# Three edits to the order of work in a fused attention and mixture-of-experts kernel: loads of k and q eight slots later, one maximum's scores ahead of the scores, the first expert's conversion later and sparser

## The chip, the cores and the metric

The kernel runs on one core of one Trainium2 chip. The metric is the device time of one execution in microseconds (us); the time before is the median of three runs. A core has five engines with a queue of instructions each: TensorE (PE, with its weight loads as PEld), VectorE (DVE), ScalarE (ACT), GpSimd (POOL) and SyncE (SP). Each executes its own instructions in their order and waits on semaphores for the others. ACT, POOL and SP also issue DMA transfers from their queues (ACTq, POOLq and SPq in the rows).

## What is computed

Masked attention over 2 batches and 8 heads (768 rows, 64 columns), then a dense layer pair with a smooth activation, then eight experts, of which each row goes to one:

```python
mask = q_bucket[:, :, :, None] == k_bucket[:, :, None, :]     # 6 sign bits of q@proj and k@proj
scores = np.where(mask, q @ k.T / 8, -1e9)
attn = exp(scores - max(scores)); attn /= attn.sum(-1) + 1e-9
x = (attn @ v)                       # as 1536 rows of 512
h = x @ w_in                         # 512 -> 2048
x = (h * tanh(log1p(exp(h)))) @ w_out
expert = argmax(normalised x @ normalised expert_emb.T)
out[row] = gate[row] * (relu(x[row] @ w1[expert]) @ w2[expert])
```

## The kernel before

Almost everything is float32 in the reference; the kernel splits each operand into two float16 parts (hi and lo) and multiplies three pairs of them on TensorE.

**Attention (from the start to about 249 us).** `run_all` walks over 16 heads. A head has six key tiles of 128 keys, and a key tile has six slots, so a head has 36 slots. All work is put at a slot number counted from slot 0 of its head; the table `AT` holds these numbers, negative ones lying in the heads before. For head n:

- `load_kq` (slot -190, now -182; every second head from the seventh on) loads k and q of two heads, two DMAs of 384 KB, from ACT's queue. `hi` (slot -150) is the first reader: an ACT instruction (L286) that writes the tile `ka`.
- `in_x` (slot -116) transposes `ka` to the tile `tx` by one DMA from SP's queue, and `args` (slot -91, L320, 12 matmuls into a PSUM tile `ar`) is its first reader. `in_m` (slot -84) transposes a tile `kq` to `tm` by a DMA from SP's queue too; the first reader is the head's first maximum unit. `load_v` (slot -37) loads v of two heads from SP's queue.
- `max_unit` computes scores for the row maxima: one matmul of 512 columns (L382) into a PSUM tile `ms`, reduced by DVE (L383, `mx`), and for every second pair of tiles two matmuls of 256 columns (L386, L387). They run ten key tiles ahead of the head's own scores. The PSUM pool `ps_m` has two buffers, which `ms` and `ar` take in turn.
- `score_unit` computes one key tile's scores: four matmuls (L422 from `tx`, L424 from `tm`) and one exponential on ACT (L427, tile `p`).
- `pv` multiplies with v, three key tiles later (L444, or L442 for the tiles that are split into two float16 parts). `out` copies a finished half to SBUF on ACT (L467, L469).

In the key tile named `first` in the code, the sixth one of a head's `pv`, slot 1 held: `pv` of the first half, `out`, the score unit of the next head, then the first maximum unit of the head three after. Such a tile comes once in each head.

Beside the heads, the weights of the dense layer are converted (`w1_work`): DVE shifts and merges them in three steps per block (L749, L751, L731), ACT rounds (L758, L759, or L765) and POOL or DVE (L766) makes the low part, into `wi` and `wo`.

**Dense layers (about 249 to 505 us).** `moe1` walks over 48 groups G, 16 for each third of the rows. In group G, PE multiplies 12 matmuls for a later group's `h` (L818, `up`), then 12 for the output of the group three before (L877). ACT and DVE evaluate the activation in between: ACT L896 (reads `h`), L901, L907, L910, then DVE L919, ACT L925, DVE L898 and L903 (the last reader of `h`), ACT L912 (`g`), POOL L913. Two PSUM buffers hold `h` in the second half of the walk, so L818 of one group waits for L903 of the group two before. After each third, ACT and DVE cut the output into parts (L949, L950, in the list `new`), and `route` follows: 16 DMA transposes from SP's queue, matmuls for the logits (L974), DVE's choice of an expert (L1012 to L1017), and a counting matmul on PE (L1025).

Side work is handed out in steps by `fill`: `every` gives how many steps stand at three places of a group (`FILL0` is 0, 3, 3, and `FILL` 0, 4, 2, so six in a group). First in the line is the rest of `w1_work`, then `w2_work`, which converts the first expert: 16 pieces, `a_0` in eight (from the loads 0 and 1) and `b_0` in eight (from the loads 2 and 3), each an ACT instruction (L1159) and a DVE instruction (L1160), one piece every `W2LAG` steps. The loads `st` come from SP's queue, into two buffers. ACT's part of a piece is put in the list `later` and issued in the middle of a group.

**Experts (about 505 us to the end).** Not touched by the change.

Of the kernel before, what the change touches and what calls it, by code (L numbers as in the profile page):

```python
# [36 lines left out]
PRE = {96: 2, 97: 2, 98: 2}  # L37
RPB, CVB = 1, 3
STEP = 7
AT = dict(rows_t=-7, rows_in=-7, m_row=-22, bits=-90, max_end=-24, hi=-150, lo0=-130, lo1=-122, dup=-114, in_x=-116, in_m=-84, args=-91, load_kq=-190, load_v=-37, out0=50, out1=54, s_row=55, inv=77, r_out=79, r_in=91, scale=112, v16=18, p16=(9, 13), xhi=127, xlo=139)  # L40
GAP = dict(bits=1, max_end=1, inv=1)
STEPS = dict(bits=3, max_end=2, inv=2)
FROM = dict(v16=2, p16=2, rows_in=1, m_row=4, bits=3, max_end=1, hi=4, lo0=4, lo1=4, dup=4, in_x=4, in_m=4, rows_t=1, args=3, load_kq=6, load_v=2)
# [3 lines left out]
SP, MP, OP = 1, (1, 5, 11), (1, 5)  # L47
# [100 lines left out]
class Attn:  # L148
# [364 lines left out]
    def run_all(self, bs, hook=None):  # L513

        seq = [(b, h) for b in bs for h in range(H)]
        N = len(seq)

        self.load_v(0, 0)
        self.load_kq(0, 2)
        act, dve = self.nc.scalar.copy, self.nc.vector.tensor_copy  # L520
        Z, pools, copies, its = self.Z, dict(s=self.ps_s, o=self.ps_o, m=self.ps_m), dict(a=act, d=dve), {}
        for line in PRO:
            f, *x = line.split()
            b, h = seq[int(x[0])] if x and f[:4] != "warm" else (0, 0)
            if f == "warm":
                self.warm(int(x[0]))
            elif f == "warm_s":
                self.warm(int(x[0]), self.ps_s.tile([P, 2, 512], F32, tag="s", name="warmed")[:, 0, 0:HS])
            elif f == "proj":
                self.proj()  # L530
            elif f == "kq":
                self.load_kq(b, h)
            elif f in ("x", "m"):
                (self.out_x if f == "x" else self.out_m)(b, h, self.turn_pe, pools[x[1]], x[1])
            elif f in ("cx", "cm"):
                Z[b, h][f](int(x[1]), copies[x[2]])
            elif f == "dup":
                self.dup(b, h, copies[x[1]])
            elif f == "args":
                self.args(b, h, pools["o"] if x[1] == "o" else None, *(int(y) for y in x[2:]))  # L540
            elif f in ("bits", "max_end"):
                if (f, h) not in its:
                    its[f, h] = getattr(self, f)(b, h)
                next(its[f, h], None)
            else:
                getattr(self, f)(b, h, *(int(y) for y in x[1:]))
        todo = {}

        def put(n, at, f, *args):
            todo.setdefault(n * NJ * 6 + at, []).append(partial(f, *seq[n], *args))  # L550

        def steps(n, f, *ats):
            def one(b, h):
                it.append(it.pop() if it else f(b, h))
                next(it[0], None)

            it = []
            for at in ats:
                put(n, at, one)

        for n in range(N):
            for name, at in AT.items():
                if n == 3:
                    at = AT3.get(name, at)
                if n == N - 1 and name in LAST:
                    continue
                if n < FROM.get(name, 0) or n >= UNTIL.get(name, N) or n % EVERY.get(name, (1, 0))[0] != EVERY.get(name, (1, 0))[1]:
                    continue
                if name == "p16":
                    for t in T16:  # L570
                        for u in range(2):
                            put(n, 6 * t + at[u], self.p16, t, u)
                elif name in GAP:
                    d = GAP[name]
                    steps(n, getattr(self, name), *(at + i * d for i in range(STEPS[name])))
                elif name == "dup":
                    put(n, at, self.dup, copies[DUPE])
                elif name in ("lo0", "lo1"):
                    put(n, at, self.lo, int(name[2]))
                elif name in ("in_x", "in_m"):  # L580
                    put(n, at, self.turn_in, name[3])
                else:
                    put(n, at, getattr(self, name))
        for k, f in (("x", self.out_x), ("m", self.out_m)):
            put(3, AT3[k], f, self.turn_pe, self.ps_m, "m")
            for i in range(2):
                copy = copies[CP3[k == "m"][i]]
                put(3, AT3[f"c{k}{i}"], lambda b, h, k, i, copy: Z[b, h]["c" + k](i, copy), k, i, copy)
        put(3, AT3["dup"], self.dup, dve)
        for g in range(G0, TEND + 1):  # L590
            n, t = divmod(g, NJ)
            m, j = divmod(g + MXL, NJ)
            p, u = divmod(g - PVL, NJ)
            if g < NJ:
                n, t = (0, S0.index(g)) if g in S0 else (-1, 0)
            if g < PVL + NJ:
                p, u = (0, O0.index(g)) if g in O0 else (-1, 0)
            for pos in range(6):
                first = g >= NJ + PVL and 0 <= p < N and u == NJ - 1
                if pos == SP and first:  # L600
                    self.pv(*seq[p], u, 0)
                    self.out(*seq[p], 0)
                if pos == SP and 0 <= n < N:
                    self.score_unit(*seq[n], t)
                if 0 <= m < N and j % 2 * 6 + pos in MP:
                    i = MP.index(j % 2 * 6 + pos)
                    self.max_unit(*seq[m], j // 2 * 2 + (i > 0), int(i == 2))
                if pos in OP and 0 <= p < N and not (first and pos == OP[0]):
                    self.pv(*seq[p], u, OP.index(pos))
                for f in todo.get(6 * g + pos, ()):  # L610
                    f()
            if hook:
                hook(g)
# [25 lines left out]
NR = CH // P  # L639
GLAG = 3  # L640
FILL = (0, 4, 2)
FILL0, SLOW = (0, 3, 3), 18
XIN = 2
AHEAD = 21
W2LAG = 6
R0, NC = 7, 10
EARLY = 48
WARM2 = (2, 2)
# [7 lines left out]
class Moe:  # L656
# [176 lines left out]
    def moe1(self, side, more):  # L833

        nc, tm = self.nc, self.tm
        N = NT // CH * NF1
        h, m, g, cuts, new = self.h, {}, {}, [], []
# [18 lines left out]
        for G in range(N + GLAG):  # L856
# [3 lines left out]
            elif G < N:  # L860
                t, w, u = m[G] = [T(tag, G) for tag in "twu"]
            new_g = 0 < G < N
            every = FILL0 if G < SLOW else FILL
            cuts, new = new[NC:], []
            ups = [2, 3, 4, 5] if G == 0 else [G + 2] if 4 <= G <= AHEAD + 1 else [G] if AHEAD + 3 < G < N else []
            if G > AHEAD:
# [2 lines left out]
            if G >= GLAG:  # L869
# [8 lines left out]
                if f == NF1 - 1:  # L878
                    route = self.route(c, x2, late, delayed)
                    if c < NT // CH - 1:  # L880
                        side.append([now + R0, route])
                        new = next(route)
# [28 lines left out]
            if old:  # L911
                nc.scalar.copy(g[G - 1][:, 0, :], p1)  # L912
                nc.gpsimd.tensor_tensor(g[G - 1][:, 1, :], p1, g[G - 1][:, 0, :], op=ALU.subtract)  # L913
            while self.later:
                self.later.pop(0)()
            for x in new[:NC]:
                x(0)
# [406 lines left out]
def moe_attn(ctx, tc, a):  # L1324
# [9 lines left out]
    with ExitStack() as c1:  # L1334
# [45 lines left out]
        with ExitStack() as c2:  # L1380
# [14 lines left out]
            with in_order(tc, last):  # L1395
                moe.busy = True
                moe.moe1([chain(work, moe.w2_work(*W[2:], W2LAG))], more)
    with ExitStack() as c2:
# [40 lines left out]
```

## Time and profile before

| what | value |
|---|---|
| time before, median of three runs | 683.24 us (682.69 to 684.28) |
| the profiled execution's own time | 685.03 us |
| its span, first to last instruction | 683.1 us |
| PE busy | 661.0 us, 97% of the span |
| ACT busy | 483.7 us, 71% |
| DVE busy | 474.7 us, 69% |
| POOL busy | 166.5 us, 24% |
| mean granted TensorE clock | 0.995 of full speed |

The profiled execution has 1.93 us around its span, and lies 1.79 us above the median of the three runs. A matmul's record includes its way through the array, so PE reads as busy over short waits: a wait shorter than about 0.16 us between two matmuls doesn't show as idle time and has to be read from the start times.

### The profile page before, as it was taken

To read this page: it belongs to the slowest core of one execution; us is meant where nothing else is said; L and a number is where in the kernel's file an instruction comes from. 1 tells how busy PE (TensorE), PEld (TensorE's weight loads), DVE (VectorE), ACT (ScalarE), POOL (GpSimd) and SP (SyncE) were. 2 spreads that over 40 slices of the span, in tenths; PEclk is the share of its full clock that TensorE was granted. 3 is DMA by queue.
4 is the path that set the end of the run, shared out by engine and by line. 5 is a ranking of instruction groups with operands and counts; after the bars stand their busy time and mean duration, and the time that the engine had idled before them with its cause. 6 is when DMAs were issued, how large, how long until landed. Compare 5 with 4: busy or idle time off the path is not lost. (4 is left out here: it accounts for less than half of the span.)

```text
span 683.1 us, 10667 instructions
## 1 busy us (share of the span) xinstructions
PE 661.0 (97%) x3946; PEld 377.8 (55%) x3946; DVE 474.7 (69%) x784; ACT 483.7 (71%) x735; POOL 166.5 (24%) x226
## 2 busy tenths in 40 slices
PE   8899999899999999999999999999999999999995
PEld 4555555455555554444444444445467777667772
DVE  7868899799988669998685665545566655566620
ACT  5667787687776779899997888887754655556530
POOL 4122122130221222322342342422522011001011
PEclk9999999999999999999999999999999999999998
DMA  7264775958563223474035010310355999999600
GB/s 222 61 144 125 154 178 132 182 142 200 126 133 109 72 76 117 123 203 152 2 94 153 1 63 0 90 36 1 103 193 167 266 280 311 265 265 259 182 23 22
DMA packets 119772, 92.72 MB, mean 136 GB/s; under 512 B 86788, under 2 KB 99076, under 8 KB 119714
## 3 DMA queue, kind: packets, MB, share of 16 engines
q1 hardware_dynamic: 111442, 80.65, 44.9%
q0 software_dynamic: 2240, 6.31, 3.4%
q10 hardware_dynamic: 6032, 5.01, 2.6%
q8 instruction: 33, 0.54, 0.4%
q14 instruction: 25, 0.20, 0.1%
HBM read 63.44 MB, written 14.24 MB: 114 GB/s over the span
## 5 line engine op out<-in xcount | busy, mean ns | idle before, releaser
L818 PE MATMUL h<-xx,wi 128*128 128x512 f16 x576 | 131.3, 379 | 0.7 <-DVE w L903 0.6
L877 PE MATMUL x<-wo,g 128*128 128x512 f16 x576 | 131.3, 379 | 0.5 <-DVE w L903 0.5
L444 PE MATMUL o<-p,vn 128*65 128x384 f32 (+3 forms) x272 | 109.4, 488 | 0.3 <-ACT su L469 0.3
L427 ACT ACTIVATE p<-s 128x768 f32<-128x768 f32 x96 | 76.8, 805 | 29.6 <-PE s L424 28.8
L877 PEld LDWEIGHTS <-g 128*128 128x128 f16 x576 | 56.3, 98 | 68.7 <-issue 0.8
L818 PEld LDWEIGHTS <-wi 128*128 128x128 f16 x576 | 56.1, 98 | 67.8 <-issue 1.1
L913 POOL TENSOR_TENSOR g<-w,g 128x512 f16<-128x512 f32 x47 | 56.9, 1210 | 148.9 <-ACT g L912 94.0
L1218 PE MATMUL y<-b,hh 128*128 128x512 f16 (+1 forms) x384 | 84.2, 379 | 0.0
L1204 PEld LDWEIGHTS <-a 128*128 128x128 f16 x768 | 75.0, 98 | 6.7 <-issue 1.6
L383 DVE TENSOR_REDUCE mx<-ms 128x1 f32<-128x512 f32 x96 | 65.3, 686 | 15.8 <-PE ms L382 15.2
L1204 PE MATMUL h<-xt,a 128*128 128x240 f16 x672 | 70.5, 266 | 1.1 <-DMA xt<-xs 1.1
L919 DVE SCALAR_TENSOR_TENSOR w<-w,u 128x512 f32<-128x512 f32 x47 | 32.4, 690 | 46.3 <-ACT u L910 44.1
L1218 PEld LDWEIGHTS <-hh 128*128 128x128 f16 (+1 forms) x384 | 43.7, 114 | 37.6
L702 DVE SCALAR_TENSOR_TENSOR b<-st,b 128x1024 f16<-128x1024 f32 x28 | 33.1, 1222 | 31.0 <-ACT b L701 31.0
L444 PEld LDWEIGHTS o<-p,vn 128*65 128x65 f32 (+1 forms) x272 | 42.5, 164 | 18.6 <-issue 8.2
L1224 POOL DMA_INDIRECT out_dram<-o,row x16 | 16.4, 1028 | 144.5 <-ACT o L1223 124.4
L424 PE MATMUL s<-tm 97*128 97x384 f16 x192 | 47.4, 327 | 0.0
L702 DVE SCALAR_TENSOR_TENSOR a<-st,a 128x1024 f16<-128x1024 f32 x28 | 34.3, 1223 | 18.8 <-ACT a L701 18.8
L422 PE MATMUL s<-tx 128*128 128x384 f16 x192 | 47.1, 327 | 0.0
L898 DVE SCALAR_TENSOR_TENSOR t<-t,u 128x512 f32<-128x512 f32 x47 | 37.8, 805 | 12.6 <-ACT t L925 12.6
L1223 ACT ACTIVATE o<-y,row 128x512 f32<-128x512 f32 (+1 forms) x16 | 11.0, 686 | 42.8 <-PE y L1218 22.8
L387 DVE TENSOR_REDUCE mx<-ms 128x2 f32<-128x512 f32 x48 | 32.9, 685 | 10.0 <-PE ms L386 9.5
(207 smaller groups left out, 1065.8 us busy)
## 6 DMA issues: line engine op xcount, KB each, us to landing
st<-in_moe_w_dram SPq DMA_DIRECT2D x32, 1024.0 KB, 5.9
stg<-in_moe_w_in_dram SPq DMA_DIRECT2D x16, 512.0 KB, 4.2
stg<-in_moe_w_out_dram SPq DMA_DIRECT2D x16, 512.0 KB, 4.2
xs<-zrow SPq DMA_DIRECT2D x15, 257.0 KB, 6.6
vn<-in_v_dram SPq DMA_DIRECT2D x16, 192.0 KB, 5.3
rb<-rd SPq DMA_DIRECT2D x14, 192.0 KB, 3.6
xr<-row SPq DMA_DIRECT2D x2, 1024.0 KB, 5.5
kq<-in_k_dram ACTq DMA_DIRECT2D x5, 384.0 KB, 4.4
```

The source lines that it names most:

```text
L383: nc.vector.tensor_reduce(z["mx"][:, j, 0:1], s, axis=AX.X, op=ALU.max)
L422: nc.tensor.matmul(s[:, c, :], kq[:, 0, ts], kq[:, 1, c * HS : (c + 1) * HS], start=True, stop=False)
L424: nc.tensor.matmul(s[:, c, :], m[0:97, 0, ts], m[0:97, 1, c * HS : (c + 1) * HS], start=False, stop=True)
L427: nc.scalar.activation(p[:, 0:S].rearrange("p (c n) -> p c n", c=2), s, AF.Exp, scale=2.0**-11)
L444: nc.tensor.matmul(o, self.vn(b, h, t), z["p"][t][:, cs], start=(t == 0), stop=(t == NJ - 1))
L702: nc.vector.scalar_tensor_tensor(lo, src, sc, hi, op0=ALU.mult, op1=ALU.subtract)
L818: self.nc.tensor.matmul(h, self.wi[wu][:, k, fs], x[:, k, xs], start=(i == 0), stop=(i == 3 * NKT - 1))
L877: nc.tensor.matmul(x2[r], gf[:, gu, rs], self.wo[wu][:, f, :], start=(f == 0 and gu + wu == 0), stop=(f == NF1 - 1 and gu == 1))
L898: nc.vector.scalar_tensor_tensor(t1, t1, 0.75, u1, op0=ALU.add, op1=ALU.mult)
L913: nc.gpsimd.tensor_tensor(g[G - 1][:, 1, :], p1, g[G - 1][:, 0, :], op=ALU.subtract)
L1204: nc.tensor.matmul(h[:, v, :], W[0][wu][:, k, fs], xt[e][:, xu * NKT + k, :], start=(i == 0), stop=(i == 3 * NKT - 1))
L1218: nc.tensor.matmul(y[s][0 : CS[s].stop - CS[s].start], hs[F // 2][:, hu, F % 2, CS[s]], W[1][wu][:, F, :], start=(F == 0 and hu + wu == 0) ...
```

## The change

Three edits. `load_kq` goes from slot -190 to -182. In the tile named `first`, the maximum unit goes ahead of the score unit. In `moe1`, the first two groups hand out no steps of side work (`QUIET`), a piece of the first expert comes every eight steps and not every six (`W2LAG`), and ACT's part of a piece isn't issued in a group that cuts an output (`not new`).

```diff
-AT = dict(rows_t=-7, rows_in=-7, m_row=-22, bits=-90, max_end=-24, hi=-150, lo0=-130, lo1=-122, dup=-114, in_x=-116, in_m=-84, args=-91, load_kq=-190, load_v=-37, out0=50, out1=54, s_row=55, inv=77, r_out=79, r_in=91, scale=112, v16=18, p16=(9, 13), xhi=127, xlo=139)
+AT = dict(rows_t=-7, rows_in=-7, m_row=-22, bits=-90, max_end=-24, hi=-150, lo0=-130, lo1=-122, dup=-114, in_x=-116, in_m=-84, args=-91, load_kq=-182, load_v=-37, out0=50, out1=54, s_row=55, inv=77, r_out=79, r_in=91, scale=112, v16=18, p16=(9, 13), xhi=127, xlo=139)
...
                     self.pv(*seq[p], u, 0)
                     self.out(*seq[p], 0)
-                if pos == SP and 0 <= n < N:
+                if pos == SP and 0 <= n < N and not first:
                     self.score_unit(*seq[n], t)
                 if 0 <= m < N and j % 2 * 6 + pos in MP:
                     i = MP.index(j % 2 * 6 + pos)
                     self.max_unit(*seq[m], j // 2 * 2 + (i > 0), int(i == 2))
+                if pos == SP and 0 <= n < N and first:
+                    self.score_unit(*seq[n], t)
...
-FILL0, SLOW = (0, 3, 3), 18
+FILL0, QUIET, SLOW = (0, 3, 3), 2, 18
...
-W2LAG = 6
+W2LAG = 8
...
-            every = FILL0 if G < SLOW else FILL
+            every = (0, 0, 0) if G < QUIET else FILL0 if G < SLOW else FILL
...
-            while self.later:
+            while self.later and not new:
                 self.later.pop(0)()
```

The instructions are the same in number on every engine. From L643 on, a line of the changed kernel has a number higher by two. The first place is ACT's queue in the seventh head, around the loads of the 13th and 14th (`kq_1_4`). Before:

```order
L427 ACTIVATE p_171<-s_6_4_1532 128x768
L276 DMA kq_1_4_1543<-in_k_dram 128x2x384
L276 DMA kq_1_4_1543<-in_q_dram 128x2x384
L758 ACTIVATE wi_102<-cv_6_1416 128x4x128
L759 ACTIVATE cv_6_1416<-cv_6_1416 128x512
L307 COPY kq_159<-ka_2_1396 128x12x64
L286 ACTIVATE ka_3_1556<-kq_1_2_1236 128x2x6x64
L427 ACTIVATE p_171<-s_6_5_1558 128x768
L427 ACTIVATE p_172<-s_7_0_1578 128x768
```

And now:

```order
L427 ACTIVATE p_171<-s_6_4_1532 128x768
L760 ACTIVATE wi_102<-cv_6_1416 128x4x128
L761 ACTIVATE cv_6_1416<-cv_6_1416 128x512
L307 COPY kq_159<-ka_2_1396 128x12x64
L286 ACTIVATE ka_3_1553<-kq_1_2_1256 128x2x6x64
L427 ACTIVATE p_171<-s_6_5_1555 128x768
L276 DMA kq_1_4_1565<-in_k_dram 128x2x384
L276 DMA kq_1_4_1565<-in_q_dram 128x2x384
L427 ACTIVATE p_172<-s_7_0_1578 128x768
```

The two loads stand behind five more ACT instructions, right after the exponential of the head's last key tile. On SP's queue nothing moves in the attention.

The second place is PE in a tile named `first`, where `pv` of the seventh head (`o_6`) ends, the eighth head's scores are made (`s_7_2`), and the maxima of the tenth begin (`ms_1_0_0` and `ms_1_1_0`, of batch 1). Before:

```order
L442 MATMUL o_6_0_1512<-p_183,vh_178 65x384
L422 LDWEIGHTS tx_7_1079
L422 MATMUL s_7_2_1619<-tx_7_1079 128x384
...
L424 MATMUL s_7_2_1619<-tm_7_1223 128x384
L382 LDWEIGHTS tm_1_1530
L382 MATMUL ms_1_0_0_1626<-tm_1_1530 128x512
...
L382 MATMUL ms_1_1_0_1632<-tm_1_1530 128x512
```

And now:

```order
L442 MATMUL o_6_0_1512<-p_183,vh_178 65x384
L382 LDWEIGHTS tm_1_1530
L382 MATMUL ms_1_0_0_1620<-tm_1_1530 128x512
L422 LDWEIGHTS tx_7_1079
L422 MATMUL s_7_2_1623<-tx_7_1079 128x384
...
L424 MATMUL s_7_2_1623<-tm_7_1223 128x384
...
L382 MATMUL ms_1_1_0_1632<-tm_1_1530 128x512
```

One matmul of 512 columns goes ahead of four of 384. DVE's order is the same in the whole attention; this happens in 12 heads.

The third place is ACT in group 24 of `moe1`, behind the square of a route (`sq_2`). Before:

```order
L912 CAST g_3961<-w_3917 128x512
L957 ACTIVATE sq_2_3906,ss_3682<-sq_2_3906 128x512
L1159 ACTIVATE b_0_2897<-st_0_3860 128x2x256
L925 ACTIVATE t_3946<-w_3947,bias_77 128x512
L896 ACTIVATE t_3975<-h_9_3978 128x512
```

And now:

```order
L914 CAST g_3951<-w_3907 128x512
L959 ACTIVATE sq_2_3898,ss_3676<-sq_2_3898 128x512
L1161 ACTIVATE a_0_2895<-st_0_3790 128x512
L927 ACTIVATE t_3936<-w_3937,bias_77 128x512
L898 ACTIVATE t_3965<-h_9_3968 128x512
```

The piece of the third load (`b_0`) that stood here is now a piece of the second (`a_0`); the first one of `b_0` stands in group 29, and the last in group 39, where it was 31. In the groups 16 to 25 ACT had ten pieces and has six now, and one rounding of `wo` more.

## Rows read from the trace of the kernel before

**Rows 1.** PE's waits: line, waited for: us in total, times, longest us.

```profile
PE ms L382 <- DMA tm<-kq: 2.0, 1, 2.0
```

**Rows 2.** Timeline, 117 to 129 us: start, us, engine, line, operation [idle before].

```profile
116.96 1.88 SPq L263 DMA_TRANSPOSE tm<-kq  x1
...
117.46 0.44 ACTq L276 DMA_DIRECT2D kq<-in_k_dram  x1
...
118.93 5.54 SPq L263 DMA_TRANSPOSE tx<-ka  x1
...
128.92 0.63 PE L382 MATMUL ms<-tm 96*128 96x512 f16 x2 [1.97 <-DMA tm<-kq]
```

**Rows 3.** Page, part 6: DMA issues, median us from issue to landing.

```profile
tx<-ka SPq DMA_TRANSPOSE x12, 5.3
```

**Rows 4.** Tile tx, 118 to 119 us: landing of its one transpose.

```profile
DMA to landing us min/median/max: 11.2/11.2/11.2
```

**Rows 5.** Tile kq, 117 to 119 us: landing of the two loads.

```profile
DMA to landing us min/median/max: 8.7/9.0/9.3
```

**Rows 6.** One window: busy time of PE, PEld, DVE, ACT, POOL, granted clock, DMA.

```profile
129.00:134.00 5.00, 5.00 (x28) 2.63 (x29) 3.77 (x10) 2.48 (x4) 0.00 (x0) 0.66 1.04 229
```

**Rows 7.** Timeline, a tile named first, 143 to 145 us.

```profile
143.18 0.49 PE L422 MATMUL s<-tx 128*128 128x384 f16 x2
...
143.75 0.16 DVE L395 TENSOR_REDUCE m<-mx 128x6 f32<-128x12 f32 x1
143.84 0.59 PE L382 MATMUL ms<-tm 96*128 96x512 f16 x2
...
144.25 0.69 DVE L383 TENSOR_REDUCE mx<-ms 128x1 f32<-128x512 f32 x1 [0.35 <-PE ms L382]
...
144.60 0.33 PE L442 MATMUL o<-p,vh 128*128 128x385 f16 x1
...
145.00 0.45 PE L320 MATMUL ar<-pj,tx 128*128 128x18 f16 x12
```

**Rows 8.** Timeline, the same place in three other heads.

```profile
73.07 0.40 PE L320 MATMUL ar<-pj,tx 128*128 128x18 f16 x10
...
86.23 0.69 DVE L383 TENSOR_REDUCE mx<-ms 128x1 f32<-128x512 f32 x1
...
199.51 0.34 PE L320 MATMUL ar<-pj,tx 128*128 128x18 f16 x8
```

**Rows 9.** All waits: ACT's for the scores.

```profile
ACT p L427 <- PE s L424: 28.8, 40, 1.9
```

**Rows 10.** Timeline, start of the dense layers.

```profile
259.95 1.65 DVE L731 SCALAR_TENSOR_TENSOR cv<-stg,cv 128x512 uint32<-128x512 uint32 x1
...
263.26 4.69 PE L877 MATMUL x<-wo,g 128*128 128x512 f16 x21 [0.50 <-DVE w L903]
```

**Rows 11.** Timeline, the first route, 367 to 388 us.

```profile
367.40 1.08 SPq L1141 DMA_DIRECT2D st<-in_moe_w_dram  x2
...
373.34 0.63 ACT L1159 ACTIVATE b<-st 128x512 f16<-128x512 f32 x1 [3.12 <-DMA st<-in_moe_w_dram]
...
381.15 2.75 PE L818 MATMUL h<-xx,wi 128*128 128x512 f16 x12 [0.62 <-DVE w L903]
...
387.47 0.17 PE L1025 MATMUL rk<-oh,tri 128*128 128x8 f16 x1 [0.97 <-DVE oh L1017]
```

**Rows 12.** Timeline, a group with a piece, and a group of the second route.

```profile
411.30 0.60 ACT L896 ACTIVATE t<-h 128x512 f32<-128x512 f32 x1 [0.61 <-PE h L818]
...
443.87 0.69 DVE L903 SCALAR_TENSOR_TENSOR w<-t,h 128x512 f32<-128x512 f32 x1
...
445.01 2.75 PE L818 MATMUL h<-xx,wi 128*128 128x512 f16 x12
```

**Rows 13.** Line 766: count, ns min/median/max, first and last start us.

```profile
L766 DVE SCALAR_TENSOR_TENSOR wo<-cv,wo x8: 691/1379/1472, 256.5 to 320.4; 128x512 f16<-128x512 f32 x8
```

**Rows 14.** Timeline of PE, the 16th group's second product.

```profile
337.74 1.46 PE L877 MATMUL x<-wo,g 128*128 128x512 f16 x6
```

## The prediction, made before the changed kernel ran

> **What bounds the kernel now.** TensorE does. The first view is the table of busy time: PE at 97% of the span, ACT and DVE near 70%. So a change can gain only where PE waits, or where its clock is low, and the second view is the list of PE's waits. Beside one at the program's start, its longest entry is a single wait of 2.0 us for the transpose `tm<-kq` [rows 1]; no other wait is over 1.0 us. The third view is the timeline at that wait: the transpose was issued at 116.96, and PE's matmul that reads it began at 128.92 after 1.97 us idle [rows 2]. The fourth is a window right behind it: over the 5.00 us from 129 to 134 the granted clock was 0.66 on average [rows 6], so part of that stretch ran at the lower of the two levels (1.2 GHz, against 2.4) after PE had stood still. Waits too short for the list are found by start times: in a tile named `first`, the last matmul of `pv` starts at 144.60, its kind takes 0.16 us from start to start, and `ar` starts only at 145.00, right after DVE's reduction of `mx` ends (144.25 + 0.69 = 144.94) [rows 7]. That is 0.24 us lost. The same place shows it in nine heads, of which the first and the last stand in [rows 8]. In the dense layers PE waits at 263.26 for 0.50 us, at 381.15 for 0.62 and at 387.47 for 0.97 [rows 10, 11], each time for DVE.
>
> All terms below come from the profiled execution: span 683.1 us, 685.03 us with what lies around it. The median of the three runs is 1.79 us lower. The first term is a late transfer, and it may be smaller in the timed runs. It can't be wholly absent there: without it the profiled execution would come to 681.3, below the lowest run (682.69). The other reading is that a profiled execution is simply longer by 1.8. I sum against 685.03 and keep the other reading for the low end.
>
> **The loads of k and q.** From 73.07 to 199.51 lie nine heads [rows 8], 126.44 us, or 122.7 without the stall and its slow stretch (1.97 + 1.70, below). That is 13.6 us for a head and 0.379 for a slot, so eight slots are 3.0 us. Before, the two loads were issued at 117.46, half a microsecond after `tm` and ahead of `tx` (118.93) [rows 2]. They took 8.7 and 9.3 us to land [rows 5], and `tx` took 11.2 [rows 4] where the median of its twelve is 5.3 [rows 3]. SP's queue was held too: the issue of `tx` alone took 5.54 us [rows 2]. Now `tm` and `tx` are both issued before the loads, which come at about 120.5. `tm` is due 10.0 us after its issue (128.92 - 1.97 - 116.96); a transpose that isn't disturbed needs about half of that.
>
> What goes: the idle 1.97 us, and of the slow stretch 5.00 x (1 - 0.66) = 1.70 us. Together 3.7. What is late next: `tx` is due 25 slots after its issue, 9.5 us, with the loads now beside its second half; and the loads themselves are due 32 slots after theirs, 12.1 us (it was 15.2), against 9.3 in the worst case seen [rows 5]. Behind an ACT instruction that waits for them stand the exponentials. The other loads of this kind, before and after, caused no wait on the list. The cost of two DMA issues on ACT stays the same and is hidden: ACT waits 28.8 us in all for PE's scores in this stage [rows 9]. Bounds of this edit: a gain of 3.7 if the stall goes and nothing else comes, none if it stays, and a loss of another stall of that size for each further load that makes one. I take 3.7.
>
> [rows 3, 4] show the loads and the transposes slowing each other although they come from two queues. The Trainium skill says the same (page "DMA: Bandwidth & Descriptors", section "Queues, rings and completion order"): each of the 16 DMA engines goes round the queues that have work, a packet at a time, so an ACT queue of its own gives the loads no separate engine. The rule speaks against this edit: the later loads still take turns with what is left of `tx`, and with the load of v behind it. If they did so as they did with `tm`, the sum would lose its first term, which is the first rival below; the trace bears this out only in part, since most loads of the kind passed without a wait.
>
> **Maxima ahead of scores.** The matmul of `ms` goes ahead of four score matmuls, which take 143.84 - 143.18 = 0.66 us [rows 7]. `ar` takes the PSUM buffer that this `ms` leaves, so it waits for DVE's reduction. DVE was idle before it for 0.35 us and free from 143.91 on (L395 ends) [rows 7]; the reduction can begin 0.34 earlier, and the 0.24 goes. In the head at 86.23 the row names no wait: DVE was busy with its own work until then [rows 8], and nothing is gained there. So 8 x 0.24 = 1.9. The exponential of that tile starts later by one matmul of 512 columns, about 0.2 us; `pv` reads it three key tiles on, and ACT has the slack of [rows 9], so it costs nothing. The first maximum unit now needs `tm` 0.66 earlier, 9.3 us after its issue: harmless if the first edit works, and 0.7 more if it doesn't. Bounds: -0.7 to 9 x 0.24 = 2.2. Against the whole 1.9 stands that DVE's order is the same and PE comes round sooner, so its next wait for DVE may take some of it back.
>
> **Side work in the dense layers.** (a) In groups 0 and 1 no steps stand between DVE's instructions for the activation; one of those before was stretched to 1.65 us [rows 10]. The wait of 0.50 us at 263.26 is for `h`'s last reader, L903, which now comes without them: 0.5 gained. The price is that all of `w1_work` comes two groups later, some 9 us. The last block of `wo` was done at about 322 [rows 13] and would be at 331, and its first reader is at 337.74 [rows 14]: hidden, with 6 us to spare. (b) At 373.34 ACT had waited 3.12 us for the load `st` of the first `b_0`, issued only at 367.40, behind the route's transposes on SP's queue [rows 11]. Every group's activation stood behind it, and 8 us later PE waited for L903 (0.62) and then for DVE's choice of an expert (0.97). Now that place holds a piece of `a_0`, whose load stands ahead of the route's transposes on SP's queue, and `b_0` begins five groups on. ACT is 3.12 us earlier, more than both waits together: 0.62 + 0.97 = 1.59 gained. (c) Seven pieces now stand in groups 32 to 39, beside the second cut and route, where there were none. A piece in a usual group is absorbed (ACT still waited 0.61 us for `h` behind one) [rows 12], but in the second route PE's L818 at 445.01 came 0.45 us after L903 ended (443.87 + 0.69) [rows 12], less than the 0.63 that a piece takes on ACT [rows 11]. I take 0.2 us lost there; the bounds are nothing and, by the waits of the first route, 1.6. The edit gives 0.5 + 1.6 - 0.2 = 1.9, between 0 and 2.1.
>
> **Sum.** 3.7 + 1.9 + 1.9 = 7.5, and 685.03 - 7.5 = 677.5 us.
>
> **The rivals.** First, the late transfer stays or moves: the loads now slow `tx` and v, or a transpose is late for another reason, and one stall of 3.7 us with its slow stretch remains. For it: one bad case in the trace had all of this in flight at once. Against: `tm` and `tx` have 3.0 us more for themselves. 677.5 + 3.7 = 681.2. Second, the short waits don't pay: what PE gains at `ar` and in the route it loses at the next wait for DVE, whose order hasn't changed. For it: DVE's reductions and conversions fill most of the attention. Only the first term is left: 685.03 - 3.7 = 681.3. Third, nothing that can be measured: the stall was rare in the timed runs, and the short waits move: about 683. Fourth, slower, by one mechanism: `tx` collides with the later loads in each pair of heads. It then lands as late as 11.2 us after its issue [rows 4] where it is due after 9.5, so `ar` waits 1.7 us, and the slow stretch (1.7) follows: 3.4 for each of the four loads in mid-attention. Three of them cost 10.2, and the time is 685.03 - 7.5 + 10.2 = 687.7; with two it is 684.3, so it decides from the third on. Against it: the median landing of `tx`, 5.3 us [rows 3].
>
> **How the numbers follow.** Chances: the forecast 0.58 (own range 675.5 to 679.5), the first rival 0.16, the second 0.13, the third 0.07, the fourth 0.06. A change within 0.2% (1.37 us, about what a measurement of this kernel can tell from none) ends at 681.87 and 684.61. The first two rivals lie just under the lower of these, and a quarter of them falls above it. So faster 0.80, no change 0.14, slower 0.06. The range goes from 675.0 (the forecast, if a profiled execution is longer by 1.8) to 682.0 (the first two rivals).
>
> **What would show it.** Right: no wait of PE for `tm<-kq` or `tx<-ka`, and no clock below full between 10 us and the end of the experts; `ar` 0.16 us behind the last `pv` matmul in most heads; no wait at the fourth matmul of L877 in `moe1`, and none of ACT for `st` in the first route. Wrong: a wait of PE for a transpose anywhere in the attention, a wait of ACT's L286 for `kq`, waits for L903 or L1017 around the second route, or PE's waits for L364 or `mx` grown by what `ar` gave up.

## The result, and the profile after

The changed kernel took 678.26 us (median of six runs, 676.44 to 678.62) beside 683.19 for the kernel before (681.83 to 686.02), a ratio of 0.9916 [0.9894, 0.9939]. Run again later it took 677.60 (676.84 to 680.02) beside 684.30, a ratio of 0.9901 [0.9881, 0.9920]. The forecast was 677.5, so the total came out. Its terms did not: the first was nearly four times too large, the other two a little too small, and the rest of the difference lay in the base of the sum, a profiled execution 1.8 us above the median.

The profiled execution of the changed kernel took 676.44 us, the lowest of its six, with a span of 674.5. From the list of PE's waits (line, waited for: us in total, times, longest):

```profile
PE warmed L230 <- POOL ones L677: 2.1, 1, 2.1
PE tm L403 <- DVE m L396: 0.7, 1, 0.7
...
PE rk L1027 <- DVE oh L1019: 0.6, 1, 0.6
PE h L820 <- DVE w L905: 0.6, 2, 0.3
```

The wait for `tm<-kq` of [rows 1] is gone; of the route waits one of 0.6 remains, the third route's. The timeline at the place of [rows 2] shows the new order of the transfers, and an `ar` that starts 0.16 us behind the last matmul of `pv`:

```profile
116.10 1.43 SPq L263 DMA_TRANSPOSE tm<-kq  x1
117.62 3.04 SPq L263 DMA_TRANSPOSE tx<-ka  x1
119.17 0.37 ACTq L276 DMA_DIRECT2D kq<-in_k_dram  x1
...
126.64 0.33 PE L442 MATMUL o<-p,vh 128*65 128x385 f16 x1
...
126.80 0.45 PE L320 MATMUL ar<-pj,tx 128*128 128x18 f16 x12
```

The landing of that `tx` (the answer to [rows 4]):

```profile
DMA to landing us min/median/max: 8.6/8.6/8.6
```

`tx` is still slow, 8.6 us where 5.3 is usual [rows 3], but in time here. The window of [rows 6] in the changed kernel (granted clock third from the right):

```profile
129.00:134.00 5.00, 4.89 (x26) 2.81 (x25) 4.78 (x6) 4.56 (x7) 1.16 (x1) 1.00 0.95 195
```

The clock is full. In the tile named `first`, as in [rows 7], the maximum's matmul now comes ahead of the scores:

```profile
138.81 0.38 PE L382 MATMUL ms<-tm 96*128 96x512 f16 x1
...
139.03 0.49 PE L422 MATMUL s<-tx 128*128 128x384 f16 x2
...
139.45 0.69 DVE L383 TENSOR_REDUCE mx<-ms 128x1 f32<-128x512 f32 x1
...
140.24 0.33 PE L442 MATMUL o<-p,vh 128*128 128x385 f16 x1
140.40 0.35 PE L320 MATMUL ar<-pj,tx 128*128 128x18 f16 x8
```

DVE's reduction ends at 139.45 + 0.69 = 140.14, before the last matmul of `pv` begins, and `ar` no longer waits for it. In the dense layers the rows that answer to [rows 10 to 12] are:

```profile
256.49 2.32 PE L879 MATMUL x<-wo,g 128*128 128x512 f16 x10
...
369.43 0.61 ACT L1161 ACTIVATE a<-st 128x512 f16<-128x512 f32 x1
...
374.25 2.75 PE L820 MATMUL h<-xx,wi 128*128 128x512 f16 x12
...
379.45 0.17 PE L1027 MATMUL rk<-oh,tri 128*128 128x8 f16 x1
...
437.90 2.75 PE L820 MATMUL h<-xx,wi 128*128 128x512 f16 x12 [0.24 <-DVE w L905]
```

The three waits of PE and ACT's wait for `st` are gone. The last row is new: PE waits beside the second route.

The time is best followed by stretches between the starts of PE's matmuls, in us: *attention 1*, from the sixth head's first `ar` to the tenth's; *attention 2*, from there to the 16th's; *start*, from the first group's second product to the 16th's; *route 1*, from the 17th's to the first matmul of group 29; *route 2*, from there to the 41st group's second product. *Late* is how much longer PE stood near 128 us than it does there with the transposes in time. *Half clock* is where the granted clock was one half for 3.4 us (the last 3 to 6 us of every kernel's span, behind its last matmuls, are left out).

| kernel | attention 1 | attention 2 | late | start | route 1 | route 2 | half clock |
|---|---|---|---|---|---|---|---|
| before | 55.29 | 85.37 | 2.13 | 75.79 | 50.05 | 76.56 | 130 |
| before_look | 55.27 | 84.34 | 2.12 | 75.79 | 50.25 | 76.55 | none |
| changed | 54.54 | 80.57 | 0 | 75.11 | 48.18 | 77.51 | none |
| after_again | 54.52 | 82.00 | 1.45 | 75.11 | 48.18 | 77.50 | none |
| a_only | 55.25 | 82.49 | 0.39 | 75.78 | 51.12 | 76.56 | 380 |
| b_only | 54.51 | 81.27 | 0.73 | 75.78 | 51.36 | 76.56 | 377, 503 |
| c_only | 55.27 | 84.64 | 2.45 | 75.11 | 48.18 | 77.17 | none |
| quiet_only | 55.26 | 83.11 | 0.92 | 75.11 | 48.18 | 76.56 | none |
| early | 55.25 | 82.09 | 0 | 75.79 | 50.81 | 76.55 | none |
| no_a | 54.52 | 82.20 | 1.65 | 75.11 | 48.18 | 77.17 | none |
| no_a_again | 54.52 | 81.08 | 0.33 | 75.11 | 48.18 | 77.17 | none |
| lag6 | 54.52 | 80.53 | 0 | 75.11 | 48.18 | 76.56 | 499 |
| lag6_again | 54.53 | 80.94 | 0.39 | 75.11 | 48.18 | 76.55 | none |
| lag6_early | 54.54 | 80.54 | 0 | 75.11 | 48.18 | 76.56 | none |

From before to changed the five stretches give -0.75, -4.80, -0.68, -1.87 and +0.95, together -7.15 of the 8.59 between the two profiled executions. The experts took 1.1 less, by waits of L1206 (L1204 before) for the DMA of `xt` that differ from run to run in every kernel, so that part is not the change's.

### The profile page after: what moved, and what is told of

Same layout as the page of the kernel before. It is cut to its first block, busy times and chain, and to the rows that moved or that the text cites. A ratio compares the mean times of both kernels' runs of the same rounds, so it can differ in the third digit from the quotient of the medians.

```text
span 674.5 us, 10665 instructions
## 1 busy us (share of the span) xinstructions
PE 657.5 (97%) x3946; PEld 376.9 (56%) x3946; DVE 480.2 (71%) x784; ACT 483.8 (72%) x735; POOL 167.8 (25%) x226
## 5 line engine op out<-in xcount | busy, mean ns | idle before, releaser
L820 PE MATMUL h<-xx,wi 128*128 128x512 f16 x576 | 131.3, 379 | 0.7 <-DVE w L905 0.6
L820 PEld LDWEIGHTS <-wi 128*128 128x128 f16 x576 | 56.1, 98 | 68.0 <-issue 1.7
L1206 PEld LDWEIGHTS <-a 128*128 128x128 f16 x768 | 75.0, 98 | 5.6 <-issue 0.5
L1206 PE MATMUL h<-xt,a 128*128 128x240 f16 x672 | 70.3, 266 | 0.2 <-DVE hh L1213 0.2
L900 DVE SCALAR_TENSOR_TENSOR t<-t,u 128x512 f32<-128x512 f32 x47 | 40.6, 863 | 9.9 <-ACT t L927 9.9
```

Of the source, the lines that this page charges most:

```text
L820: self.nc.tensor.matmul(h, self.wi[wu][:, k, fs], x[:, k, xs], start=(i == 0), stop=(i == 3 * NKT - 1))
L900: nc.vector.scalar_tensor_tensor(t1, t1, 0.75, u1, op0=ALU.add, op1=ALU.mult)
L1206: nc.tensor.matmul(h[:, v, :], W[0][wu][:, k, fs], xt[e][:, xu * NKT + k, :], start=(i == 0), stop=(i == 3 * NKT - 1))
```

## The experiments

The theory after the first result: the late transfer differs from run to run, so the loads are worth less than 3.7, and the rest more than 3.8. The rival is the prediction's own split. The first four runs did one edit at a time, on one chip, beside 683.87 for the kernel before.

**The loads alone.**

```diff
-load_kq=-190
+load_kq=-182
```

> The kernel before with the loads of k and q eight slots later and nothing else. First theory (the loads slow the transposes that were issued beside them, in every execution): no wait of PE for tm or tx, no stretch at the lower clock in the attention, the waits of 0.24 us at ar stay; 3 to 3.7 us less than the kernel before, about 679.8. Rival (the late transpose was an accident of the profiled execution, rare in the timed runs): within 0.7 us of the kernel before. Second rival (the loads now slow tx): PE waits for tx at ar in at least one head.

Measured: 682.88 (680.83 to 684.14), ratio 0.9987 [0.9971, 1.0003]. The timeline of this kernel at two places, and one window:

```profile
128.62 0.46 PE L320 MATMUL ar<-pj,tx 128*128 128x18 f16 x12 [0.46 <-DMA tx<-ka]
...
379.11 2.44 PE L818 MATMUL h<-xx,wi 128*128 128x512 f16 x7 [1.12 <-DVE w L903]
```

```profile
380.00:383.00 3.00, 3.00 (x8) 1.06 (x7) 2.21 (x3) 2.07 (x4) 1.94 (x2) 0.50 0.00 0
```

The wait for `tm` is gone and a small one for `tx` has come, as the prediction's first rival had it. The half clock that stood behind the wait for `tm` in [rows 6] stands behind the first route's wait here. A gain of about 1 in the median, not 3.7.

**The maxima alone.**

```diff
-if pos == SP and 0 <= n < N:
+if pos == SP and 0 <= n < N and not first:
...
+if pos == SP and 0 <= n < N and first:
+    self.score_unit(*seq[n], t)
```

> The kernel before with the first maximum unit ahead of the score unit in the tile named first, and nothing else. First theory: the 0.24 us at ar go in eight of nine heads, 1.5 to 1.9 us less, about 681.4; where the transpose tm is late, PE stands still ahead of the scores instead of behind them, up to 0.7 us longer. Rival (the time is lost again at the next wait for DVE): as much wait at L364 or at mx as ar gave up, time within 0.5 us of before.

Measured: 681.07 (679.97 to 684.44), ratio 0.9967 [0.9948, 0.9986]. The waits of `ar` for DVE were gone but for 0.13 us in the head at 87 us. Everywhere else but at the late transfer `ar` stands 0.16 us behind the last matmul of `pv`, as here:

```profile
154.43 0.33 PE L442 MATMUL o<-p,vh 128*65 128x385 f16 x1
154.59 0.45 PE L320 MATMUL ar<-pj,tx 128*128 128x18 f16 x12
```

PE did not give the time back: attention 1 took 54.51 where it had taken 55.29.

**The side work alone**, with all its parts, and then the quiet groups alone, with the lag left at six.

```diff
-FILL0, SLOW = (0, 3, 3), 18
+FILL0, QUIET, SLOW = (0, 3, 3), 2, 18
...
-W2LAG = 6
+W2LAG = 8
...
-every = FILL0 if G < SLOW else FILL
+every = (0, 0, 0) if G < QUIET else FILL0 if G < SLOW else FILL
...
-while self.later:
+while self.later and not new:
```

> The kernel before with the three changes to the side work of the dense layers and nothing else. First theory: the wait at the fourth matmul of L877 goes (0.5 to 0.7), those for L903 and L1017 in the first route go (1.6 to 1.9), and waits for L903 of about 1.0 in all come in groups 35 to 40 of moe1, where the last pieces of the first expert now stand: 1.5 us less, about 681.7. Rival: the first expert's pieces just move their cost, with as much waiting in the second route as went in the first.

> The kernel before with no side work in groups 0 and 1 and nothing else: a piece every six steps as before, pieces also in a group that cuts. The first piece of b_0 comes in group 26 instead of 24, the last in group 33, so ten pieces still stand in groups 18 to 27. First theory (ACT's wait of 3.12 us for the load of b_0 made PE's two waits in the first route): ACT doesn't wait for st, the waits for L903 and L1017 in the first route go, none come in the second: 2.3 to 2.5 us less, about 680.8. Rival (the pieces stood too close, whatever the load did): both waits stay at 0.5 us or more each, and the gain is the 0.5 to 0.7 us at the fourth matmul of L877.

Measured: 681.33 (679.82 to 682.59), ratio 0.9961 [0.9947, 0.9975], and for the quiet groups alone 680.82 (678.85 to 683.12), ratio 0.9957 [0.9936, 0.9977]. The first route is the same in both (48.18). In the second only the eight-step lag costs (77.17 against 76.56). ACT's wait for `st` in the first route was 3.12, 3.30, 3.62, 3.98 and 3.59 us in before, before_look, a_only, b_only and early. With the quiet groups alone the piece there is one of `a_0` and doesn't wait. The load of `b_0` is issued 12.4 us before its first piece, which doesn't wait either:

```profile
365.17 9.57 SPq L1141 DMA_DIRECT2D st<-in_moe_w_dram  x2
...
373.00 0.61 ACT L1159 ACTIVATE a<-st 128x512 f16<-128x512 f32 x1
377.56 0.63 ACT L1159 ACTIVATE b<-st 128x512 f16<-128x512 f32 x1
```

So the load of `b_0` caused the waits of the first route, and moving it by two groups was enough: neither the lag nor the rule on `new` was needed. With c_only PE stood idle for the transpose, longer than before, and yet the clock stayed full in the window of [rows 6]:

```profile
129.69 0.64 PE L382 MATMUL ms<-tm 96*128 96x512 f16 x2 [2.29 <-DMA tm<-kq]
...
129.00:134.00 5.00, 4.24 (x31) 2.60 (x32) 3.83 (x11) 2.38 (x4) 0.00 (x0) 1.00 1.03 232
```

**The kernel before once more, and with the loads much earlier.** The second one has them 24 slots ahead, so that they have landed when the transposes begin.

```diff
-load_kq=-190
+load_kq=-214
```

> The kernel before once more, for one profile. Theory: the stall at the fourth load (near 129 us) is there again, with another size between 0.5 and 2.5 us, and the stretch of half clock (3.4 us long) stands somewhere behind a wait of PE, not always behind this one. Rival, the prediction's reading: the same two, 1.97 us of idle and the half clock right behind it.

> The kernel before with the loads of k and q at slot -214 and not -190, some 9 us earlier: they have landed before the transposes tm and tx of that place are issued. Theory: the stall near 129 us comes from the loads' packets beside the transposes'. Then neither tm nor tx is late, no wait of PE over 0.3 us stands between 126 and 133 us, and the transposes there land 5 to 6 us after their issue; the time is 0.9 to 1.5 us below the kernel before, ratio 0.9978 to 0.9987. Rival: the transposes are late for another reason at that place (the load of a block of the dense weights issued just ahead of them on SP's queue, or the fetch of instructions at 125 us); then a wait of 0.5 to 2.5 us stays and the ratio is 0.999 to 1.001. Second rival: the earlier loads collide with the transposes of the head before (issued at 103 to 105 us) and the stall moves there.

Measured: 684.02 for the first, one run. Its list of waits has the wait for `tm` at the same size, so the first theory's spread of sizes was not seen in this one:

```profile
PE ms L382 <- DMA tm<-kq: 2.0, 1, 2.0
```

The half clock is missing behind it. With the loads early: 681.87 (681.44 to 682.60), ratio 0.9965 [0.9950, 0.9980], a gain of 2.0, more than expected and twice that of the edit. Its timeline and the landing of `tx`:

```profile
107.90 0.38 ACTq L276 DMA_DIRECT2D kq<-in_k_dram  x1
...
118.61 2.85 SPq L263 DMA_TRANSPOSE tx<-ka  x1
```

```profile
DMA to landing us min/median/max: 5.8/5.8/5.8
```

So the loads' packets beside the transposes' made the wait; the load of dense weights ahead of them and the fetch of instructions were there in this run too. Its 12 runs spread over 1.2 us, those of the kernel before over 5.0: much of the kernel's own scatter came with this transfer, and with the half clock that goes with it (counted below).

**The change without its first edit, and without the longer lag.** Then both again on one chip with the changed kernel, and a fourth kernel with the lag of six and the early loads.

```diff
-load_kq=-182
+load_kq=-190
```

> The changed kernel with the loads of k and q back at slot -190. Theory: in the timed runs the later loads are worth about 0.9 us, as the run with them alone gave (ratio 0.9987), since the stall at the fourth load is smaller there than the 1.97 us with a half-clock stretch of 1.70 that one profile showed: about 679.2, ratio 0.994. In the profile PE waits 0.5 to 2.5 us near 128 us for the transposes tm or tx. Rival, the prediction's term: 3.7 us, so 682.0, ratio 0.998, with a stretch of half clock behind the stall. Second rival: worth nothing, 678.3.

```diff
-W2LAG = 8
+W2LAG = 6
```

> The changed kernel with a piece of the first expert every six steps, as before; the rest of the change stays. Theory: the lag of eight buys nothing in the first route (QUIET alone and the rule on new outputs do that) and puts seven pieces beside the second route, where the changed kernel's profile has new gaps of PE of 0.51 (427.1) and 0.40 (437.9). Then the stretch from the group after the second cut (up29) to its end is 76.5 to 76.6 us long and not 77.5, and the time is 0.6 to 1.0 us below the changed kernel's 678.26: about 677.4, ratio to the kernel before 0.9898 to 0.9910. Rival: the waits in the first route (381 to 388) come back, because pieces stand denser there; then that stretch (from 336 to 386 us) is 50.0 us and not 48.2, and the time 679 to 680.

> The changed kernel once more, on the same chip as the next three. Theory: 678.3, with no wait for tm or tx of over 0.3 us near 128 us, the two new waits of L820 (0.5 and 0.4 us, near 427 and 438), and at most one stretch of half clock (3.4 us, about 1.5 lost) somewhere behind a wait in the routes. Rival: its stall near 128 us comes back in some executions, then the runs spread over more than 2.2 us.

> The changed kernel with the loads at slot -190, on the same chip as the changed kernel. The first run gave 678.81 in another call, whose ratio (0.9917) is that of the changed kernel (0.9916). Theory: its profile lost 1.63 us between the tenth and the 16th head's first ar (82.20 against 80.57), with no half clock, so in one call it is 1.0 to 1.8 us above the changed kernel. Rival by the ratios: 0 to 0.5 above. Rival by the prediction: 3.7 above.

> The changed kernel with a piece every six steps, on the same chip as the changed kernel. Theory: 0.95 us below it, by the stretch around the second route (76.56 against 77.51). The two medians of different calls were 1.6 apart. Rival: 1.6 or more, if a wait in the second route also draws a stretch of half clock.

> The same with the loads of k and q at slot -214, ahead of the transposes and not behind them. Theory: tx lands in 5 to 6 us and not 8.7 at the fourth load; no wait is left there to remove, so the median is the same within 0.3 us, and the runs spread less (the kernel before with the early loads had 1.2 us from the lowest to the highest of 12, and 5.0 with its own). Rival: the loads at slot -182 still cost a wait in other executions than the profiled one; then it is 0.5 to 1.0 us faster. Second rival: the earlier loads collide with the transposes of the head before; then slower.

| kernel | us (range) | ratio to before |
|---|---|---|
| no_a | 678.81 (677.44 to 679.55) | 0.9917 [0.9892, 0.9942] |
| lag6 | 676.64 (676.38 to 677.90) | 0.9893 [0.9869, 0.9918] |
| after_again | 677.60 (676.84 to 680.02) | 0.9901 [0.9881, 0.9920] |
| no_a_again | 678.38 (677.18 to 682.88) | 0.9930 [0.9909, 0.9952] |
| lag6_again | 676.93 (676.47 to 678.11) | 0.9891 [0.9873, 0.9910] |
| lag6_early | 676.61 (676.20 to 677.22) | 0.9889 [0.9870, 0.9908] |

The last four shared a chip. There the first edit is worth 678.38 - 677.60 = 0.78 in the median, less than expected. That figure is uncertain: the ratios of the same two kernels would make it 2.0, and those of the first pair (0.9917 for no_a, 0.9916 for the changed kernel) nothing. The expectation that the changed kernel has no wait at 128 us failed; the timeline of its second profile, the highest of its six runs, shows:

```profile
128.56 0.46 PE L320 MATMUL ar<-pj,tx 128*128 128x18 f16 x12 [1.29 <-DMA tx<-ka]
```

So its rival held: the edit makes the stall smaller and rarer, and doesn't remove it. The lag of six gained 0.67 in the median, where the stretches say 0.95; where L820 waited at 437.90, it doesn't now:

```profile
435.58 0.69 DVE L905 SCALAR_TENSOR_TENSOR w<-t,h 128x512 f32<-128x512 f32 x1
...
436.73 2.75 PE L820 MATMUL h<-xx,wi 128*128 128x512 f16 x12
```

The rival that pieces at six steps would bring the first route's waits back fell (48.18). The fourth kernel, the lag of six with the early loads, has the lowest median, 1.0 us below the changed kernel. The intervals of the two ratios overlap, so that is not shown beyond the noise, but it has the narrowest range of the four. Against lag6_again it gained 0.3, as expected.

## Why the prediction was right in the total and wrong in its parts

**The loads: the step that failed.** "What goes: the idle 1.97 us, and of the slow stretch 5.00 x (1 - 0.66) = 1.70 us. Together 3.7." By medians the edit is worth 0.99 alone and 0.78 within the change, and alone its interval reaches no change. Both halves were mis-sized. Over the seven profiles with the loads at -190, PE was late by 10.33 / 7 = 1.48 us, and over the five at -182 still by 2.23 / 5 = 0.45: the difference is 1.03, an estimate, since single profiles lie between 0.33 and 2.45 and between 0 and 1.45. And the slow stretch was priced too high: before and before_look were late by the same 2.13 and 2.12, and *attention 2* differs by 85.37 - 84.34 = 1.03, which is what the stretch cost in time, not the 1.70 read from the clock. Nor did it belong to the wait: of the seven profiles one had it there, so at that place it is worth some 0.15 on average. In lag6 it came behind the last route's wait of 0.59, in a_only and b_only behind the first route's (in b_only again at 503 us). The price of one execution's slow stretch was put on the edit whole.

**What was late next** was named rightly: `tx`, due 9.5 us after its issue. It landed after 8.6 to 9.9 in the five profiles with the loads at -182. The first rival ("the loads now slow `tx`") was thus half true. The packets of the two loads, in the window from 116 to 128 us (packets, MB, share of the 16 engines' time), of before:

```profile
q10 hardware_dynamic: 544, 0.79, 34.1%
```

and of the changed kernel:

```profile
q10 hardware_dynamic: 544, 0.79, 17.7%
```

The same packets took about half the time. The Trainium skill's rule that the engines go round the queues a packet at a time (page "DMA: Bandwidth & Descriptors", section "Queues, rings and completion order") had spoken for that rival. The traces agree as to the slowing; the order of single packets was not read. With more distance it goes: at -214 `tx` took 5.8. The fourth rival, a collision in each pair of heads, fell: no other load made PE wait.

**The maxima** were right and slightly small: 1.9 forecast. By stretches they are worth 55.29 - 54.54 = 0.75 and, with no late transfer on either side, 82.09 (early) - 80.54 (lag6_early) = 1.55, together 2.30; the ratio of b_only gives 2.3 too. The rows counted as nine heads hold ten such waits, since the first and the last both count, and the one at 86 us that was written off gained as well. The second rival, that the waits don't pay, fell.

**The side work.** (a) 0.5 forecast, 0.68 measured. (b) 1.59 forecast, 50.05 - 48.18 = 1.87 measured against the same profile, and 2.07 to 3.18 against the other four with that wait: it was bigger in most executions than in the one read, and twice drew the half clock. The cause named, the load `st` of `b_0`, is shown by quiet_only. (c) 0.2 lost was forecast, 0.95 measured: inside the bounds of 0 to 1.6, but the value stood near the wrong end. Waits for L903 around the second route were one of the prediction's own signs of being wrong, and they came. The rows that it had read spoke for more: L818 started 0.45 after L903's end, a piece takes ACT 0.63, and two groups beside the second route lost 0.51 and 0.40. Only the first of them, with 0.61 in the whole stretch, stands in all five profiles with eight steps. The second came only in the two that also have the loads at -182. In both of these DVE's part of the piece there took 1.02 (the first row below, of the changed kernel), in the other three 0.69 (the second, of no_a_again), and L905 ended later by as much. What stretched it is not shown.

```profile
434.54 1.02 DVE L1162 SCALAR_TENSOR_TENSOR b<-st,b 128x512 f16<-128x512 f32 x1 [0.54 <-ACT b L1161]
...
434.55 0.69 DVE L1162 SCALAR_TENSOR_TENSOR b<-st,b 128x512 f16<-128x512 f32 x1 [0.89 <-ACT b L1161]
```

**The total.** From 685.03 the terms were 3.7 + 1.9 + 1.9. Measured they are about 1.0, 2.3 and 2.3 (0.68, plus 2.54 as the mean of five first routes, less 0.95; the ratio of c_only gives 2.7), together 5.6. From the medians of before, 683.19 and 684.30, that leads to 677.6 and 678.7, where 678.26 and 677.60 were measured. The profiled execution lay 1.8 above its median, and the sum took the late transfer and the slow stretch of that one execution off as the edit's gain. The stretch is about 1.0 of the 1.8: before_look, with the same wait at full clock, took 684.02. "It can't be wholly absent there" was wrong as an argument: half-size waits and slow stretches elsewhere fill the timed runs as well. The two errors cancelled, which was luck. Two small slips in the sums change nothing: the nine heads are 122.8 us, and the reason given for the low end of the range leads to 675.7, not 675.0.

Does the half clock also come more seldom in the changed kernel? The mean granted clock of each timed run tells. The ten profiled executions without a stretch have 0.996 to 0.998, the four with one or two have 0.991 to 0.995. A clock of 0.994 or less is found in:

| kernel | runs at 0.994 or less |
|---|---|
| before, beside the other runs | 27 of 67 |
| early | 0 of 12 |
| a_only | 5 of 12 |
| b_only | 6 of 12 |
| quiet_only | 5 of 12 |
| c_only | 3 of 12 |
| changed kernel, both times | 0 of 12 |
| no_a and no_a_again | 2 of 16 |
| lag6 and lag6_again | 1 of 12 |
| lag6_early | 0 of 6 |

So it does. None of the edits alone brings it about, while the early loads alone do; which of the edits together do it is not shown. That fits a gain of early at twice the edit's. The top of the scatter goes with it too: the 17 runs of the kernel before at 0.993 or less have a median of 686.27 us, the 31 at 0.996 or more one of 683.04.

## What to carry to other kernels

A wait for a transfer, and a slow-clock stretch behind it, are one draw from a distribution: look at a second profile, and take such a term by its mean, not from the execution that happened to be recorded. A wait of one engine for another in a fixed order (here `ar` for DVE's reduction, 0.24 each) came out in every profile to 0.1 us, and such a term can be summed. One that has a transfer behind it can't: the first route's waits for DVE, behind the load of `b_0`, cost 1.87 to 3.18. To keep two transfers apart, move the one with slack well ahead of the other rather than a little behind it: 24 slots ahead took the wait away here, eight slots behind only made it smaller.

## What was not expected of the hardware

A half-clock stretch of 3.4 us (granted clock 0.50, so 1.2 GHz) stood in four of 14 profiles, at 130, 377, 380, 499 and 503 us, each time in or just behind a wait of PE. But equal waits passed without one: 1.96 us of idle in before_look and 2.29 in c_only, at the place of [rows 1] at full clock. In lag6 it followed a wait of only 0.59 and matmuls of 8 columns:

```profile
498.19 0.17 PE L1027 MATMUL rk<-oh,tri 128*128 128x8 f16 x1 [0.59 <-DVE oh L1019]
...
496.00:504.00 8.00, 7.41 (x83) 5.96 (x80) 4.58 (x24) 2.74 (x9) 2.60 (x3) 0.79 0.19 69
```

What decides it stays open. The other surprise is how much of a kernel's scatter one transfer can carry: 5.0 us from lowest to highest with the loads among the transposes, 1.2 without.
